# Turning more score blocks in place of computing them, with z, q and the output buffers rearranged (gated attention and hypermixer MLP, one core)

## The chip, the cores and the metric

The kernel runs on one core of one Trainium2 chip. The metric is the device time of one execution in microseconds (us). The kernel before was timed three times: 807.54, 807.89 and 812.27 us, with a median of 807.89 us.

A core has five engines that run their own instruction lists in order: PE (TensorE, the matmuls), DVE (VectorE), ACT (ScalarE), POOL (GpSimd) and SP (SyncE, which here only issues DMA transfers). They meet through semaphores. A DMA that SP issues is run by 16 DMA engines; SP itself takes some time to issue it, and cannot issue the next before.

## The reference

There are 8 batches of 3200 rows. The first part is an attention without a softmax, and the second mixes its result with two projections of itself:

```python
scores = (1.0 / S) * np.matmul(z, z.transpose(0, 2, 1))   # z: 8 x 3200 x 64
attn = np.maximum(scores, 0.0) ** 2                       # 8 x 3200 x 3200
x = u * np.matmul(attn, v)                                # u, v, x: 8 x 3200 x 256
wq = x @ w_q                                              # 8 x 3200 x 64
wk = x @ w_k
mixed = np.einsum('bst,btd->bsd', scale * np.einsum('bsd,btd->bst', wq, wk), x)
out = np.maximum(mixed, 0.0) @ w_out                      # 8 x 3200 x 256
```

The scores are symmetric, since both factors are z. What is computed for (row block i, column block j) is, transposed, the block (j, i).

## The kernel before

**Tiles and groups.** A batch has 25 row tiles of 128 (`NT`). The columns are cut into seven groups, six of 512 and a last one of 128 (`widths`, `LASTG`). A score tile is one row tile against one group: 128 x 512. Two tiles share a pair: `scores` (L210) computes both with two matmuls that use the two halves of the PE's rows, into one PSUM tile `sc`. `first_stage` (L229 on ACT, L233 on DVE) takes max(x, 0) and scales into the fp32 tile `g`; `second_stage` (L246 on ACT, L248 on POOL) squares `g` into the fp16 tile `at`.

**Turned blocks.** `is_turned(gi, gj)` says which blocks are computed only once: those of group gi against the rows of a later group gj, where gj is at most `FAR = 2` groups on, or is the last group. `second_stage` gives each such pair of tiles to SP, which issues a DMA transpose (L267) into a tile `tt1`, `tt2` or `ttl`. When group gj's turn comes, its missing rows are read from there (`weights`).

**Steps.** The main loop (`while groups`) runs in steps, counted by `k`. A step computes three pairs of score tiles (two where it also mixes), runs the first stage of these, the second stage of the pairs of the step before, and then a share of the second product (L288: attn times v, 25 row tiles x 4 column blocks for a group of 512) with tiles that are two steps old (`LAG = 2`). A batch takes 21 steps, 169 steps in all. When a group closes, `gate` (L314, DVE) multiplies by u into `x_sb`, and `turn_x` (L326) has SP transpose it into `xT`.

**Keys and queries.** Five or more steps later, in a step that neither mixes nor follows another such step too closely (`key_due`), `keys_and_heads` projects the group (L336), ACT casts it into `qk` (L347: rows 0 to 63 are q, 64 to 127 are k), and SP transposes it into `kx` (L352). At the next such step, here called a key step, `double_keys_queries` copies q into the other half of `qk` by a DMA of SP (L360) and k into the other half of `kx` by POOL (L361), and `heads` (L367, PE) needs that `kx`. So the key transpose has from one key step to the next to land. Once a whole batch has its heads, `mix` (L415), `mix_out` (L427, ACT), `proj` (L440) and `proj_out` (L464, and L465 for the store) run for one of its groups every third step, during the next batch.

**z of the next batch** (`group_begun`): `load_z` (L130) loads all of it with a cast to fp16 by a DMA of POOL's queue, 3 steps after the batch's first group begins; `double_z` (L133, DVE) doubles it 6 steps later, and `turn_z` (L137) has SP transpose all 25 tiles in one instruction one step after that. v comes in five pieces of POOL's queue (L126).

**Order on SP.** SP has a plain list, in the order in which the loop calls it: in each step first what is due (`at_phase`: u, z), then q copies, then the transposes of the second stage, stores and key transposes. An instruction of SP that waits holds all that are behind it.

**Buffers.** `pg` has 8 buffers of 4 KB a partition, which `g` shares with the output tiles `fo` and `fs`. The 14 buffers of `pat` hold `at`.

Of the kernel before, what the change touches and what calls it, by code (L numbers as in the profile page):

```python
# [9 lines left out]
FP16 = mybir.dt.float16  # L10
# [6 lines left out]
def kernel(  # L17
# [10 lines left out]
    nc = tc.nc  # L28
# [13 lines left out]
    LAG = 2  # L42
    FAR = 2

# [14 lines left out]
    pu = ctx.enter_context(tc.tile_pool(name="pu", bufs=2))  # L59
    pg = ctx.enter_context(tc.tile_pool(name="pg", bufs=8))  # L60
    pat = ctx.enter_context(tc.tile_pool(name="pat", bufs=NAT))
# [22 lines left out]
    ZCH = [(0, 4), (12, 6), (18, 7), (4, 8)]  # L84
    ident = consts.tile([P, P], FP16, tag="ident", name="ident")
    z32 = {}
    zd0 = pz.tile([P, NT, 2, dqk], FP16, tag="zd", name="zd")
    vs[0] = pv.tile([P, NT, D], FP16, tag="v_sb", name="v_sb")
# [10 lines left out]
    def cast_first(c):  # L99
        n0, nn = ZCH[c]  # L100
        casts = [
            (nc.vector.tensor_copy, nc.scalar.copy),
            (nc.scalar.copy, nc.gpsimd.tensor_copy),
            (nc.gpsimd.tensor_copy, nc.gpsimd.tensor_copy),
            (nc.gpsimd.tensor_copy, nc.gpsimd.tensor_copy),
        ][c]
        for half, cast in enumerate(casts):
            cast(out=zd0[:, n0 : n0 + nn, half, :], in_=z32[n0][:])

    def turn_first(c):  # L110
        n0, nn = ZCH[c]
        if c < 2:
            tp = acc_tile(c, "ztp", FP16)
        else:
            tp = pps.tile([P, 4 * W], FP16, tag="ps", name="ztp")
        for i in range(nn):
            nc.tensor.transpose(  # L117
                tp[:, ts(i, P)], zd0[:, n0 + i, :, :].rearrange("p a k -> p (a k)"), ident
            )
        copy = nc.scalar.copy if c == 1 else nc.vector.tensor_copy  # L120
        copy(out=zT[0][:, ds(n0 * P, nn * P)], in_=tp[:, 0 : nn * P])
# [5 lines left out]

    def load_z(b):
        zds[b] = pz.tile([P, NT, 2, dqk], FP16, tag="zd", name="zd")
        nc.gpsimd.dma_start(out=zds[b][:, :, 0, :], in_=rows(z, b))  # L130

    def double_z(b):
        nc.vector.tensor_copy(out=zds[b][:, :, 1, :], in_=zds[b][:, :, 0, :])  # L133

    def turn_z(b):
        zT[b] = pzt.tile([P, S], FP16, tag="zT2", name="zT2")
        nc.sync.dma_start_transpose(  # L137
            out=zT[b][:].rearrange("p (n s) -> p n s", s=P),
            in_=zds.pop(b)[:].rearrange("p n a k -> p (n a k)"),
        )  # L140
# [6 lines left out]

    wq32 = consts.tile([P, ND, dh], FP32, tag="wq32", name="wq32")
    wk32 = consts.tile([P, ND, dh], FP32, tag="wk32", name="wk32")
    wqk = consts.tile([P, ND, 2, dh], FP16, tag="wqk", name="wqk")  # L150
    wq2 = consts.tile([P, ND, 2, dh], FP16, tag="wq2", name="wq2")
    wk2 = consts.tile([P, ND, 2, dh], FP32, tag="wk2", name="wk2")
    wo = consts.tile([P, ND, D], FP16, tag="wo", name="wo")
    wo32 = {}

    def load_weights():
        wo32[0] = px.tile([P, ND, D], FP32, tag="x_sb", name="wo32")
        nc.sync.dma_start(out=wq32[:], in_=moe_w_q.rearrange("(c p) h -> p c h", p=P))
        nc.sync.dma_start(out=wk32[:], in_=moe_w_k.rearrange("(c p) h -> p c h", p=P))
        nc.sync.dma_start(out=wo32[0][:], in_=moe_w_out.rearrange("(c p) e -> p c e", p=P))  # L160

    def cast_weights():
        nc.gpsimd.tensor_copy(out=wqk[:, :, 0, :], in_=wq32[:])
        nc.gpsimd.tensor_copy(out=wqk[:, :, 1, :], in_=wk32[:])
        for half in range(2):
            nc.gpsimd.tensor_copy(out=wq2[:, :, half, :], in_=wq32[:])
            nc.gpsimd.tensor_copy(out=wk2[:, :, half, :], in_=wk32[:])
        nc.gpsimd.tensor_copy(out=wo[:], in_=wo32[0][:])

# [5 lines left out]

    def is_turned(gi, gj):
        return gi < gj and (gj <= gi + FAR or gj == LASTG)

# [7 lines left out]
    for b in range(B):  # L186
        for gi in range(NG):
            near = [t for t in range(NT) if is_turned(gi, group_of(t))]
            own = [
                t for t in range(NT) if t not in near and not is_turned(group_of(t), gi)  # L190
            ]
            if b == 0 and gi == 0:
                order = [t for n0, nn in ZCH for t in range(n0, n0 + nn)]
                assert sorted(order) == sorted(near + own)
            elif len(tiles) % 2:
                order = own[:1] + near + own[1:]
            else:
                order = near + own
            tiles += [(b, gi, t) for t in order]
            ends[b, gi] = len(tiles)  # L200
# [38 lines left out]
    def second_stage(p0, g, on_act):  # L239
# [11 lines left out]
        for tile_ in tiles[p0 : p0 + 2]:  # L251
            b, gi, ti = tile_
            made[tile_] = (at, at0)
            gj = group_of(ti)
            if is_turned(gi, gj):
                blocks.append((b, gi, gj, ti - starts[gj] // P, 1, at0, at0 + widths[gi]))
            at0 += widths[gi]
        if len(blocks) == 2 and blocks[0][:3] == blocks[1][:3] and blocks[1][3] == blocks[0][3] + 1:
            blocks = [blocks[0][:4] + (2, blocks[0][5], blocks[1][6])]
        for b, gi, gj, n0, nn, c0, c1 in blocks:  # L260
            if (b, gi, gj) not in turned:
                kind, nr, bufs = ("l", 1, 8) if gj == LASTG else (gj - gi, 4, gj - gi + 2)
                turned[b, gi, gj] = ptt.tile(
                    [P, nr, 4, P], FP16, tag=f"tt{kind}", name=f"tt{kind}", bufs=bufs
                )
            out = turned[b, gi, gj][:].rearrange("p n j t -> p (n j) t")
            nc.sync.dma_start_transpose(out=out[:, 4 * n0 : 4 * (n0 + nn), :], in_=at[:, c0:c1])  # L267
# [55 lines left out]
    def turn_x(b, gi):  # L323
        nn = widths[gi] // P
        xTs[b, gi] = pxt.tile([P, 4, ND, P], FP16, tag="xT_sb", name="xT_sb")
        nc.sync.dma_start_transpose(  # L326
            out=xTs[b, gi][:, 0:nn, :, :].rearrange("p n a s -> p (n a) s"),
            in_=xs[b, gi][:, 0:nn, :].rearrange("p n d -> p (n d)"),
        )
# [14 lines left out]
    def projections_out(b, gi, out):  # L344
        gw = widths[gi]
        qks[b, gi] = pq.tile([P, W], FP16, tag="qk", name="qk")
        nc.scalar.copy(out=qks[b, gi][:, 0:gw], in_=out)  # L347
# [8 lines left out]

    def double_keys_queries(b, gi):
        gw = widths[gi]
        nn = gw // P
        nc.sync.dma_start(out=qks[b, gi][dh:P, 0:gw], in_=qks[b, gi][0:dh, 0:gw])  # L360
        nc.gpsimd.tensor_copy(out=ks[b, gi][:, 0:nn, 0, :], in_=ks[b, gi][:, 0:nn, 1, :])  # L361
# [87 lines left out]
    def proj_out(b, gi, src, ways):  # L449

        n0 = starts[gi] // P
        fo = pg.tile([P, 2, W], FP32, tag="g", name="fo")
        flat_out = fo[:].rearrange("p a w -> p (a w)")
# [49 lines left out]
    def side_proj_out(b, ps):  # L503
        fo = pg.tile([P, 2, W], FP32, tag="g", name="fs")
        nc.scalar.mul(out=fo[:, 0, 0:D], in_=ps[:, 1, D : 2 * D], mul=FINAL_SCALE)
        nc.sync.dma_start(out=rows(out, b)[:, NT - 1, :], in_=fo[:, 0, 0:D])

# [3 lines left out]

    def due(k, fn):
        at_phase.setdefault(k, []).append(fn)

# [9 lines left out]
    def keys_and_heads(b, gis):  # L524
# [15 lines left out]
        if keyed:  # L540
            hb, hgis = keyed.pop(0)
            heads_out(hb, hgis, ps)
            if hgis[-1] == LASTG:
                todo_mix.extend((hb, i) for i in range(LASTG))
                side.append((side_mix, side_mix_out, hb))
        if aside:
            aside[1](aside[2], ps)
# [3 lines left out]
    def group_begun(k, b, gi):  # L551
# [4 lines left out]
        if gi == 0 and b + 1 < B:  # L556
            later = 4 if b == 0 else 0
            due(k + later + 3, lambda: load_z(b + 1))
            due(k + later + 9, lambda: double_z(b + 1))
            due(k + later + 10, lambda: turn_z(b + 1))  # L560
            for i in range(5):
                due(k + later + 5 + 3 * i, lambda i=i: load_v(b + 1, 5 * i, 5))

# [33 lines left out]
    while groups:  # L597
# [17 lines left out]
        if keying and keyed:  # L615
            for g_ in keyed[0][1]:
                double_keys_queries(keyed[0][0], g_)
        if mixing:
# [3 lines left out]
        for i, (p0, sc) in enumerate(fresh):  # L622
            on_act = i == act_pair and not mixing
            staged.append((p0, first_stage(p0, sc, on_act)))
        if k < 3:
            turn_first(k + 1)
# [86 lines left out]
    for g_ in hgis:  # L713
        double_keys_queries(hb, g_)
    psh = ps_tile("hd")
    heads(hb, hgis, psh, stop=False)
    last_gram(last, LASTG, psg)
    g32 = pg.tile([P, ND * D], FP32, tag="g", name="G")
# [4 lines left out]
    last_heads(last, g32, psh)  # L723
    heads_done(last, psh[:, 1, 0:D])
    for mb, mg in todo_mix[2:]:
        mix_out(mb, mg, mix(mb, mg))
# [53 lines left out]
```

## Time and profile before

| | |
|---|---|
| three runs, us | 807.54, 807.89, 812.27 |
| profiled execution, us | 811.74 |
| its span (first to last instruction), us | 810.0 |
| busy us: PE, DVE, ACT, POOL | 790.2, 492.0, 475.1, 485.5 |
| score matmuls (L210) | 920, busy 130.6 us |
| matmuls of the second product (L288), all three sources | 5000 |
| DMA transposes issued by SP: `tt`, `ttl`, `xT_sb`, `kx`, `zT` | 146, 48, 56, 54, 7 |
| granted TensorE clock | 1.00 throughout |

The profiled execution is 3.85 us longer than the median of the three runs, about as long as the slowest. Busy time of the PE is a sum over stretches in which at least one matmul was in flight. A row of the page's fifth part gives a group of instructions: line, engine, operation, output and inputs, count, then busy time and mean length of one, then the idle time of that engine just before and what ended it.

### The profile page before, as it was taken

How to read it: one execution, taken by the hardware profiler on the slowest of the kernel's cores; microseconds unless marked ns; L12 is line 12 of the kernel's file. 1: busy time of each engine (PE TensorE's matmuls, PEld its weight loads, DVE VectorE, ACT ScalarE, POOL GpSimd, SP SyncE). 2: the span in 40 equal slices, each digit the busy share in tenths (PEclk: the TensorE clock that was granted, in tenths of full speed). 3: DMA queues.
4: the chain of work that ended last, by engine and by line, in shares of the span. 5: the costliest groups of instructions: out<-in, count | busy, mean ns of one | idle time of the engine just before them, and what ended most of it. 6: DMA issues, size and time to landing. Idle time of an engine off the chain costs nothing.

```text
span 810.0 us, 16777 instructions
## 1 busy us (share of the span) xinstructions
PE 790.2 (98%) x6778; PEld 585.3 (72%) x6778; DVE 492.0 (61%) x514; ACT 475.1 (59%) x526; POOL 485.5 (60%) x352
## 2 busy tenths in 40 slices
PE   7999999999999999999999999999999989999996
PEld 4777777777777777777777777777777757767774
DVE  5766666656665556745666556755666646655525
ACT  6655555556665556555665556656665555565534
POOL 7966676564766457745666466764666555655410
PEclk9999999999999999999999999999999999999999
DMA  7999899997999969998999979999899996868536
GB/s 174 153 206 187 140 177 169 207 195 133 216 148 193 206 169 177 149 231 172 187 153 212 198 156 176 178 210 178 188 200 151 174 221 138 157 136 194 119 95 247
DMA packets 330877, 143.20 MB, mean 177 GB/s; under 512 B 307440, under 2 KB 313136, under 8 KB 330800
## 3 DMA queue, kind: packets, MB, share of 16 engines
q1 hardware_dynamic: 302528, 125.90, 76.5%
q0 software_dynamic: 28128, 15.98, 18.6%
q8 instruction: 53, 0.87, 0.5%
q14 instruction: 24, 0.20, 0.1%
q10 hardware_dynamic: 144, 0.26, 0.1%
HBM read 59.38 MB, written 26.21 MB: 106 GB/s over the span
## 4 chain that ended last, share of the span: by engine, by line
PE 91%; DMA 3%; DVE 2%; ACT 1%; issue 1%; SPq 1%; POOL 1%; DVEq 0%; POOLq 0%; ACTq 0%
PE acc L288 65%; PE sc L210 13%; PE fo L440 5%; PE qk L336 3%; PE qk L367 2%; DMA out_dram<-fo 2%; PE mx L415 2%; DVE g L233 1%; SPq L267 1%; POOL at L248 1%; ACT at L246 1%; PE ztp L117 0%; DMA xT_sb<-x_sb 0%; DVE x_sb L314 0%; DMA z<-in_z_dram 0%
## 5 line engine op out<-in xcount | busy, mean ns | idle before, releaser
L248 POOL TENSOR_TENSOR at<-g 128x1024 f16<-128x1024 f32 (+2 forms) x234 | 430.5, 1855 | 213.8 <-DVE g L233 124.5
L233 DVE TENSOR_SCALAR g<-sc 128x1024 f32<-128x1024 f32 (+1 forms) x340 | 388.1, 1184 | 193.9 <-PE sc L210 157.3
L288 PE MATMUL acc<-v_sb,at 128*128 128x256 f16 x3656 | 446.8, 273 | 0.4 <-DVE x_sb L314 0.4
L288 PEld LDWEIGHTS <-at 128*128 128x128 f16 x3656 | 344.7, 98 | 107.4 <-issue 66.6
L229 ACT ACTIVATE g<-sc 128x1024 f32<-128x1024 f32 x128 | 131.2, 1025 | 199.0 <-PE sc L210 186.7
L246 ACT ACTIVATE at<-g 128x1024 f16<-128x1024 f32 (+2 forms) x234 | 236.9, 1029 | 0.6 <-DVE g L233 0.6
L288 PE MATMUL acc<-v_sb,tt 128*128 128x256 f16 x1152 | 149.1, 273 | 0.0
L210 PE MATMUL sc<-zT 64*128 64x512 f16 x920 | 130.6, 382 | 4.6 <-DVE g L233 2.1
L288 PEld LDWEIGHTS <-tt 128*128 128x128 f16 x1152 | 112.5, 98 | 12.9
L314 DVE TENSOR_TENSOR x_sb<-acc,u_sb 128x512 f16<-128x512 f32 (+1 forms) x104 | 69.3, 668 | 66.9 <-PE acc L288 62.8
L427 ACT ACTIVATE rt<-mx 128x1024 f16<-128x1024 f32 (+1 forms) x49 | 49.1, 1012 | 56.8 <-PE mx L415 55.3
L210 PEld LDWEIGHTS <-zT 64*128 64x128 f16 x920 | 35.2, 95 | 53.4 <-issue 30.8
L361 POOL COPY kx<-kx 128x256 f16<-128x256 f16 (+1 forms) x54 | 20.1, 377 | 78.5 <-DMA kx<-qk 74.8
L464 ACT ACTIVATE fo<-fo 128x1024 f32<-128x1024 f32 (+1 forms) x40 | 40.6, 1014 | 27.2 <-PE fo L440 26.0
L440 PE MATMUL fo<-wo,rt 128*128 128x256 f16 x386 | 49.6, 273 | 1.9 <-ACT rt L427 1.0
L347 ACT CAST qk<-qk 128x512 f16<-128x512 f32 (+1 forms) x54 | 28.7, 545 | 28.5 <-PE qk L367 13.2
L440 PEld LDWEIGHTS <-rt 128*128 128x128 f16 x386 | 37.2, 98 | 7.8 <-ACT rt L427 2.2
L380 DVE TENSOR_TENSOR ha<-ha,qk 128x256 f32<-128x256 f32 x31 | 13.1, 421 | 30.1 <-ACT qk L347 30.1
L367 PE MATMUL qk<-x_sb,kx 128*128 128x256 f16 x191 | 28.4, 273 | 2.7 <-POOL kx L361 2.7
L336 PE MATMUL qk<-xT_sb,wqk 128*128 128x512 f16 (+1 forms) x108 | 29.9, 358 | 0.2
L367 PEld LDWEIGHTS <-kx 128*128 128x128 f16 x195 | 19.0, 98 | 15.0 <-POOL kx L361 3.2
L288 PE MATMUL acc<-v_sb,ttl 128*128 128x256 f16 x192 | 22.6, 273 | 0.0
(47 smaller groups left out, 149.4 us busy)
## 6 DMA issues: line engine op xcount, KB each, us to landing
u_sb<-in_u_dram SPq DMA_DIRECT2D x48, 512.0 KB, 4.8
out_dram<-fo SPq DMA_DIRECT2D x46, 512.0 KB, 4.3
v_sb<-in_v_dram POOLq DMA_DIRECT2D x35, 320.0 KB, 6.2
qk<-qk SPq DMA_DIRECT2D x47, 64.0 KB, 4.2
zd<-in_z_dram POOLq DMA_DIRECT2D x7, 400.0 KB, 8.0
tt<-at SPq DMA_TRANSPOSE x146, 4.5
u_sb<-in_u_dram SPq DMA_DIRECT2D x8, 128.0 KB, 3.1
xT_sb<-x_sb SPq DMA_TRANSPOSE x56, 3.9
```

Of the source, the lines that this page charges most:

```text
L210: nc.tensor.matmul(out=sc[:, h, 0:gw], lhsT=zT[b][half : half + dqk, ts(ti, P)], rhs=zT[b][half : half + dqk, ds(gs, gw)], start=True, sto ...
L229: nc.scalar.activation(out=g[:, hs, 0:w], in_=sc[:, hs, 0:w], func=RELU, scale=GSCALE)
L233: nc.vector.tensor_scalar(out=g[:, hs, 0:w], in0=sc[:, hs, 0:w], scalar1=0.0, scalar2=GSCALE, op0=AOP.max, op1=AOP.mult,)
L246: nc.scalar.square(out=out, in_=g[:, hs, 0:w])
L248: nc.gpsimd.tensor_mul(out=out, in0=g[:, hs, 0:w], in1=g[:, hs, 0:w])
L288: nc.tensor.matmul(out=accs[j // 2][:, ds((j % 2) * D, D)], lhsT=weights(b, gi, ti, j), rhs=vs[b][:, ti, :], start=(first and ti == rows_[ ...
L314: nc.vector.tensor_mul(out=xs[b, gi][:, 2 * half : 2 * half + n, :].rearrange("p n d -> p (n d)"), in0=accs[half][:, 0 : n * D], in1=us[b, ...
L336: nc.tensor.matmul(out=out, lhsT=w[:, ac, :, :].rearrange("p t h -> p (t h)"), rhs=xTs[b, gi][:, 0 : gw // P, ac, :], start=(start and ac ...
L367: nc.tensor.matmul(out=ps[:, 1, 0:D], lhsT=ks[b, gi][:, n, :, :].rearrange("p a h -> p (a h)"), rhs=xs[b, gi][:, n, :], start=((gi, n) == ...
L427: nc.scalar.activation(out=rts[b, gi][:, :, 0:gw], in_=ps[:, :, 0:gw], func=RELU)
L440: nc.tensor.matmul(out=banks[jf // 2][:, ds((j - jf) * D, D)], lhsT=rt[:, dc, ts(j, P)], rhs=wo[:, dc, :], start=(dc == 0 and j == jf), st ...
L464: nc.scalar.mul(out=flat_out[:, sl], in_=part, mul=FINAL_SCALE)
```

## The change

- `is_turned` takes the batch too: in all batches but the last a block three groups on is turned as well, which adds the blocks (0,3), (1,4) and (2,5) and a third kind of tile, `tt3`. The numbers of buffers are 3, 4 and 3.
- The order of the tiles within a group changes: the tiles of the next group come first, then the group's own, then the other turned ones; tile 24 is put first or last, so that pairs stay together.
- z of the next batch is loaded as fp32 by SP in four pieces (6, 6, 6 and 7 tiles), each cast twice by DVE two steps later, after the first stages of that step (`late`), and turned by SP one step after that.
- q is copied into its other half by DVE (`double_queries`), before the group is mixed, and not by SP.
- Outputs have buffers of their own (`pfo`); `g` has 7 buffers and shares them only after the main loop. `xT` and `qk` of the last group get small buffers of their own, and the weights are staged in `px`.

```diff
-    def is_turned(gi, gj):
-        return gi < gj and (gj <= gi + FAR or gj == LASTG)
+    def is_turned(b, gi, gj):
+        far = 3 if b + 1 < B else 2
+        return gi < gj and (gj <= gi + far or gj == LASTG)
...
-            elif len(tiles) % 2:
-                order = own[:1] + near + own[1:]
             else:
-                order = near + own
+                single = [NT - 1]
+                order = [t for t in near if group_of(t) == gi + 1 < LASTG]
+                order += [t for t in own + near if t not in order + single]
+                order = single + order if len(tiles) % 2 else order + single
...
-    def load_z(b):
-        zds[b] = pz.tile([P, NT, 2, dqk], FP16, tag="zd", name="zd")
-        nc.gpsimd.dma_start(out=zds[b][:, :, 0, :], in_=rows(z, b))
+    def load_z(b, i):
+        n0, nn = ZP[i]
+        z32[b] = pz.tile([P, 7, dqk], FP32, tag="z32", name="z32")
+        nc.sync.dma_start(out=z32[b][:, 0:nn, :], in_=rows(z, b)[:, n0 : n0 + nn, :])
...
+        for half in range(2):
+            nc.vector.tensor_copy(out=zds[b][:, 0:nn, half, :], in_=z32[b][:, 0:nn, :])
...
-        nc.sync.dma_start(out=qks[b, gi][dh:P, 0:gw], in_=qks[b, gi][0:dh, 0:gw])
+    def double_queries(b, gi):
+        gw = widths[gi]
+        nc.vector.tensor_copy(out=qks[b, gi][dh:P, 0:gw], in_=qks[b, gi][0:dh, 0:gw])
...
-        fo = pg.tile([P, 2, W], FP32, tag="g", name="fo")
+        if groups:
+            fo = pfo.tile([P, 2, W], FP32, tag="fo", name="fo")
+        else:
+            fo = pg.tile([P, 2, W], FP32, tag="g", name="fo")
...
-            due(k + later + 3, lambda: load_z(b + 1))
-            due(k + later + 9, lambda: double_z(b + 1))
-            due(k + later + 10, lambda: turn_z(b + 1))
+            for i in range(4):
+                due(k + later // 4 + 2 + 3 * i, lambda i=i: load_z(b + 1, i))
+                due(k + later // 4 + 4 + 3 * i, lambda i=i: double_z(b + 1, i), late)
+                due(k + later // 4 + 5 + 3 * i, lambda i=i: turn_z(b + 1, i))
             for i in range(5):
-                due(k + later + 5 + 3 * i, lambda i=i: load_v(b + 1, 5 * i, 5))
+                due(k + later + 3 + 3 * i, lambda i=i: load_v(b + 1, 5 * i, 5))
```

## The prediction

> **What bounds the kernel now.** I read the page's busy times first, then the groups of instructions, then the waits, then SP's own timeline.
>
> ```profile
> span 810.0 us, 16777 instructions
> PE 790.2 (98%) x6778; PEld 585.3 (72%) x6778; DVE 492.0 (61%) x514; ACT 475.1 (59%) x526; POOL 485.5 (60%) x352
> ...
> L210 PE MATMUL sc<-zT 64*128 64x512 f16 x920 | 130.6, 382 | 4.6 <-DVE g L233 2.1
> ...
> L361 POOL COPY kx<-kx 128x256 f16<-128x256 f16 (+1 forms) x54 | 20.1, 377 | 78.5 <-DMA kx<-qk 74.8
> ```
>
> The PE is busy 98% of the span, and none of the other three engines is near that. So what takes matmuls away shortens the kernel, as long as nothing else falls behind. The last row shows what is nearest to that: POOL stood 74.8 us for key transposes. The list of waits says how often, and who else waits:
>
> ```profile
> POOL kx L361 <- DMA kx<-qk: 74.8, 19, 9.4
> ...
> DVE g L233 <- DMA out_dram<-fo: 21.9, 7, 5.2
> ...
> PE qk L367 <- POOL kx L361: 2.7, 1, 2.7
> ...
> PE sc L210 <- DVE g L233: 2.1, 3, 0.8
> ```
>
> Each line gives the total in us, the number of times and the longest. Key transposes were late for POOL 19 times, and late for the PE once, by 2.7 us. So the slack is nearly spent. The reason is in SP's timeline of the third batch (start, time, instructions merged):
>
> ```profile
> 210.08 4.51 SPq L267 DMA_TRANSPOSE tt<-at  x2
> ...
> 224.52 10.71 SPq L267 DMA_TRANSPOSE tt<-at  x4
> ...
> 239.27 2.50 SPq L352 DMA_TRANSPOSE kx<-qk  x1
> ...
> 246.77 5.05 SPq L137 DMA_TRANSPOSE zT<-zd  x1
> ...
> 278.28 0.63 SPq L145 DMA_DIRECT2D u_sb<-in_u_dram  x1
> ```
>
> Between 210 and 279 us of that batch each instruction starts 0.1 us after the one before has ended: SP is never idle. It is the second bound of this kernel, for some 60 of a batch's 98 us. What it costs to issue is in the views of the tiles `tt` and `qk` (least, median and longest, ns):
>
> ```profile
> L267 SPq DMA_TRANSPOSE tt<-at x146: 1212/1290/6540, 20.5 to 750.5; - x146
> L352 SPq DMA_TRANSPOSE kx<-qk x54: 1108/1223/3109, 53.7 to 779.0; - x54
> L360 SPq DMA_DIRECT2D qk<-qk x54: 467/554/1582, 65.7 to 789.7; - x54
> ```
>
> A transpose takes SP 1.29 us, and longer where the DMA engines are full: the 146 sum to 250.4 us, a mean of 1.72. In the stretch above the mean is 1.84.
>
> **Part by part.**
>
> *Turned blocks.* Three block pairs of four tiles in seven batches are 84 score tiles less (920 to 836), and 169 steps become 155. L210 is busy 130.6 us for 920, or 0.142 us each with two in flight: 84 x 0.142 = **11.9 us less on the PE**. DVE, ACT and POOL lose 84/920 of their stages: about 35, 34 and 39 us, off the path and worth nothing by themselves.
>
> *Output buffers.* The 21.9 us that DVE stood for a store's landing end, since `g` no longer waits for stores. The PE's own row gives 2.1 us for waits on DVE before scores: **2.1 us less**.
>
> *q and z on DVE.* 54 copies and 56 casts are added; one doubling in seven batches (8.4 us) goes. Nearest rows: the doubling took 0.58 us alone and up to 2.19 us, and the first cast of 128x256 took 0.29 us. At some 0.38 us that is 42 us on DVE, against 35 + 8 us less: no change to its 61%. I take 0; hidden by DVE's 157 us of waits for scores. A cast that waits for late z would hold gates and first stages behind it. Its z is issued two steps earlier (8 to 11 us), SP is up to 12 us late, and the first loads of z landed in 2.1 to 5.4 us, so this can be late by about 5 us in the same stretch where SP is late anyway; I count it in the next part and let the upper end carry the rest.
>
> *SP's list.* I counted SP's instructions in the built program's order for groups 0 to 3 of the third batch (62.8 us before, 196.8 to 259.6), where the load is. Each price has 0.1 us added for the gap.
> - Transposes of `at`: 18 become 26. 8 x 1.82 = +14.6.
> - z transposes: one of 5.05 becomes three pieces (the fourth falls in group 4) of 6 tiles, nearest to the 8-block `tt` at its median: 3 x 1.39 - 5.15 = -1.0.
> - z loads: 4 x 0.52 = +2.1 (the first loads took 0.40 to 0.43). One more store: +0.5.
> - q copies: 5 less, mean 0.66 (31.2 us for 47): -3.8.
> - z by POOL's queue: its 128-byte packets ran from 209 to 214 us, and the two transposes beside and behind them took 3.18 and 2.19 us against 1.25: -2.8.
> Sum +9.6 us. The PE's time for these groups shrinks by 0.8 us (13 tiles for 17 in group 3), so SP has 10.4 us more to make up. From 196 to 210 us SP stood idle for 5.5 us in pieces; if it can use all of it, it ends about **5 us later** than before against the PE.
>
> What is late then is a key transpose. In batches three to six the one in group 2 was issued 10.4, 13.2, 10.1 and 10.9 us after the start of its key step, mean 11.2. That cost nothing, since the next key step came 25 us later. In the changed program key steps come every third step nearly throughout; here these have 6, 6 and 7 row tiles, and such steps took 4.3 (with keys), 4.1 (with a mix) and 3.9 us: 12.3 us. How late an issue may be: 13.7 us was just met with 15.3 us to the next key step, and at 640 us the same 13.7 with 14.5 made the PE wait 2.7. So about 1.5 us less than the distance: 10.8 here. With 5 us more, 16.2 - 10.8 = 5.4 us of waiting; as part of the 5 us is issued behind that transpose, I take 4 us a batch. The first batch has no stores or mixes yet, and the eighth turns no more than before: six batches, **24 us more**. Bounds: at the unloaded 1.39 in place of 1.82 the sum is 6.2 and the lag 1.5 us, a wait of about 1.7 us a batch, 10 us in all; at the saturated 1.94 and with nothing saved on z, some 10 us a batch, 60 us, though each wait gives SP time to catch up. And 0, if transposes of keys now stand earlier in the list than I count.
>
> **Sum.** 811.7 - 11.9 - 2.1 + 24 = 821.7 us for the profiled execution. That stands 3.85 us above the median of the three runs, so 818 us in their terms.
>
> **Rivals.**
>
> *The backlog is absorbed.* Turned tiles of the next group come first in a step's list now, one 5 us transpose and POOL's slow z are gone, and SP issues for only 623 of 810 us. Then only the gain stays: 807.9 - 14 = 794 to 799. Against it stands that groups 0 to 3 hold nearly all that is added, and that groups 4 to 6 get none of it. Point at which it decides: a key transpose issued under about 11 us after its step's start. Chance 0.25.
>
> *The new copies of DVE collide with POOL.* Three of the seven doublings took 0.58 us with POOL idle; the four that met a multiply of POOL's took 0.95 to 2.19, and two of those multiplies 2.20 in place of 1.88. A mean of 0.61 us more on 110 copies is 67 us on DVE, 492 to 559 us, and 7 us of POOL. If a tenth or so of it comes before a gate or a first stage that the PE needs, that is 7 to 10 us: 794 + 10 = 804, no measurable change. The Trainium skill, SBUF — State Buffer, Who interferes with whom, has this as a rule that speaks against the move: VectorE in its two-port modes (copies and casts among them) and GpSimd exclude each other, and the second to start waits for the whole instruction. The doublings agree with that, 2.19 us beside a multiply of 1.88; whether the new casts run in such a mode no run here shows yet. Chance 0.08.
>
> *SP and the DMA engines saturate.* The 84 tiles bring 43,008 packets of 256 bytes (302,528 on SP's queue before); in the table by windows the DMA share over groups 1 to 3 of the third batch is 0.85, 1.07 and 1.09 already (packets in flight overlap, so it can pass 1). If issue goes to 1.94 us throughout, half of the 60 us above arrives: 830 to 850. Chance 0.25.
>
> **Chances.** The forecast (811 to 828) has 0.42, of which 0.27 lies above 816 and 0.15 within 1% of 807.9. About 1% either way is what a measurement of this kernel can tell from no change, as the runs lie 4.4 us apart. Faster by over 1%: 0.25, from the first rival. Within 1%: 0.15 + 0.08 = 0.23. Slower: 0.27 + 0.25 = 0.52. The range runs from 795 to 842 us and leaves out the best of the first rival and the worst of the third. The signs are mixed; the forecast's own range is 811 to 828.
>
> **What would show it.** Right: L210 falls to 836 matmuls and about 119 us; the PE's waits for `kx` by POOL (L361) grow from 2.7 us to over 15; SP without idle time from group 0 to group 4; DVE's waits for stores gone. Wrong: PE waits for `kx` near zero and a span near 798 (absorbed), or waits of the PE on `g` and `x_sb` with copies of q and z of 1 us and more (the collision). A wait of DVE's casts for z would be a step that I counted in the wrong place.

## The result, and the profile after

The changed kernel takes 863.24 us (median of 6 runs, 857.52 to 870.62) against 807.71 us (median of 6, 806.06 to 812.27): 1.0656 times as long, with a 95% interval from 1.0626 to 1.0687. I had forecast 818 us and a range up to 842. The direction was right, the size was not: 55 us instead of 10. Times here and below are medians of all runs of a kernel, while ratios leave out a run that lies over 1.5% above the kernel's fastest (one each of after, `a_z_old`, `b_dummy8`, `a_24zact` and `a_ord2`), so that a difference of two times can be 2 us more than the ratios give: by the ratio, 53 us here.

The profiled execution after took 857.52 us, so it is the fastest of its six runs, 5.7 us under their median; what follows explains 46 of the 55 us. These lines of its page answer to those shown of before (busy time of each engine, then groups of instructions; a line number is now some 11 to 19 higher):

```profile
span 855.7 us, 16629 instructions
...
PE 796.6 (93%) x6694; PEld 590.0 (69%) x6694; DVE 533.3 (62%) x587; ACT 439.9 (51%) x495; POOL 437.8 (51%) x323
...
PEclk9999899999999899999999999999999999999999
...
L221 PE MATMUL sc<-zT 64*128 64x512 f16 (+1 forms) x836 | 120.4, 382 | 20.2 <-DMA zT<-zd 15.0
...
L380 POOL COPY kx<-kx 128x256 f16<-128x256 f16 (+1 forms) x54 | 21.0, 390 | 165.3 <-DMA kx<-qk 161.7
...
L376 DVE COPY qk<-qk 64x512 f16<-64x512 f16 x48 | 46.4, 972 | 1.2
...
L138 DVE CAST zd<-z 128x384 f16<-128x384 f32 (+1 forms) x56 | 31.6, 605 | 15.4 <-DMA z<-in_z_dram 15.3
```

The 84 score matmuls are gone (836), and the PE is still busy for 6 us more than before, in a span that is 46 us longer. POOL stands 161.7 us for key transposes, before 74.8. And two lines are new: VectorE's copies of q at 0.97 us each, and its casts of z, which themselves wait 15.3 us for z. The PE's own waits (total, times, longest) tell which of this reaches it:

```profile
PE sc L221 <- DMA zT<-zd: 15.0, 3, 6.6
PE qk L386 <- POOL kx L380: 13.9, 11, 2.9
PE acc L299 <- DVE x_sb L325: 8.5, 13, 2.7
PE mx L434 <- DVE qk L376: 3.9, 4, 1.8
PE sc L221 <- ACT rs L509: 3.8, 2, 3.3
```

Before, the largest but one of all such lines was the 2.7 us for `kx`. Now the PE waits 15.0 us for turned pieces of z, in three waits only; 13.9 us for doubled keys; and 8.5 us for gates, `x_sb`, which VectorE makes.

For the rest I took the start-to-start time of every pair of successive matmuls. Its median for the same two lines is the undisturbed pace; what a pair takes beyond it is a pause, or, where the trace's clock record reads 0.50, time lost to the clock. From the first matmul's start to the last's:

| us | before | after |
|---|---|---|
| undisturbed pace | 785.4 | 775.6 |
| pauses | 12.9 | 55.7 |
| lost at half clock | 0 | 14.2 |
| small differences | 2.4 | 0.9 |
| sum | 800.7 | 846.4 |

The removed matmuls are worth 9.8 us. Pauses cost 42.8 us more, nearly all in the five lines above, and the half clock 14.2 us that no line of waits shows. These are estimates: how the pairs are sorted moves pace and pauses by up to 7 us against each other, and the half clock by about 2.

### The profile page after: what moved, and what is told of

Read it like the earlier page. It is cut to its first block, busy times and chain, and to the rows that moved or that the text cites. A ratio compares the mean times of both kernels' runs of the same rounds, so it can differ in the third digit from the quotient of the medians.

```text
span 855.7 us, 16629 instructions
## 1 busy us (share of the span) xinstructions
PE 796.6 (93%) x6694; PEld 590.0 (69%) x6694; DVE 533.3 (62%) x587; ACT 439.9 (51%) x495; POOL 437.8 (51%) x323
## 4 chain that ended last, share of the span: by engine, by line
PE 72%; issue 8%; DMA 7%; DVE 5%; POOL 5%; SPq 1%; ACT 1%; DVEq 0%; POOLq 0%; ACTq 0%
PE acc L299 52%; PE sc L221 9%; PE fo L459 4%; POOL at L259 4%; PE qk L386 3%; DMA z<-in_z_dram 2%; DMA kx<-qk 2%; PE qk L350 2%; DVE g L244 2%; PE mx L434 1%; DMA zT<-zd 1%; DVE x_sb L325 1%; DVE qk L376 1%; DMA ttl<-at 1%; DVE zd L138 1%
## 5 line engine op out<-in xcount | busy, mean ns | idle before, releaser
L259 POOL TENSOR_TENSOR at<-g 128x1024 f16<-128x1024 f32 (+1 forms) x212 | 391.7, 1863 | 218.6 <-DVE g L244 111.3
L244 DVE TENSOR_SCALAR g<-sc 128x1024 f32<-128x1024 f32 (+2 forms) x309 | 356.3, 1194 | 167.6 <-PE sc L221 166.5
L299 PE MATMUL acc<-v_sb,at 128*128 128x256 f16 x3320 | 414.3, 276 | 8.8 <-DVE x_sb L325 8.5
L299 PEld LDWEIGHTS <-at 128*128 128x128 f16 x3320 | 316.3, 99 | 111.2 <-issue 71.0
L240 ACT ACTIVATE g<-sc 128x1024 f32<-128x1024 f32 (+2 forms) x117 | 116.0, 994 | 228.6 <-PE sc L221 219.5
L299 PE MATMUL acc<-v_sb,tt 128*128 128x256 f16 x1488 | 189.8, 276 | 0.0
L299 PEld LDWEIGHTS <-tt 128*128 128x128 f16 x1488 | 147.5, 99 | 18.9
L221 PE MATMUL sc<-zT 64*128 64x512 f16 (+1 forms) x836 | 120.4, 382 | 20.2 <-DMA zT<-zd 15.0
L380 POOL COPY kx<-kx 128x256 f16<-128x256 f16 (+1 forms) x54 | 21.0, 390 | 165.3 <-DMA kx<-qk 161.7
L221 PEld LDWEIGHTS <-zT 64*128 64x128 f16 x836 | 32.2, 95 | 69.2 <-issue 33.7
L376 DVE COPY qk<-qk 64x512 f16<-64x512 f16 x48 | 46.4, 972 | 1.2
L386 PE MATMUL qk<-x_sb,kx 128*128 128x256 f16 x191 | 29.6, 279 | 13.9 <-POOL kx L380 13.9
L138 DVE CAST zd<-z 128x384 f16<-128x384 f32 (+1 forms) x56 | 31.6, 605 | 15.4 <-DMA z<-in_z_dram 15.3
```

What stands on the lines that cost most here:

```text
L221: nc.tensor.matmul(out=sc[:, h, 0:gw], lhsT=zT[b][half : half + dqk, ts(ti, P)], rhs=zT[b][half : half + dqk, ds(gs, gw)], start=True, sto ...
L240: nc.scalar.activation(out=g[:, hs, 0:w], in_=sc[:, hs, 0:w], func=RELU, scale=GSCALE)
L244: nc.vector.tensor_scalar(out=g[:, hs, 0:w], in0=sc[:, hs, 0:w], scalar1=0.0, scalar2=GSCALE, op0=AOP.max, op1=AOP.mult,)
L259: nc.gpsimd.tensor_mul(out=out, in0=g[:, hs, 0:w], in1=g[:, hs, 0:w])
L299: nc.tensor.matmul(out=accs[j // 2][:, ds((j % 2) * D, D)], lhsT=weights(b, gi, ti, j), rhs=vs[b][:, ti, :], start=(first and ti == rows_[ ...
L376: nc.vector.tensor_copy(out=qks[b, gi][dh:P, 0:gw], in_=qks[b, gi][0:dh, 0:gw])
```

## Experiments

Each time below stands beside runs of the kernel before on the same chip (medians of 807.7 to 809.1 us); the ratio is to those. "Far" is how many groups ahead blocks are turned.

### Which part costs it: the third group, z, or q

Five kernels take the change apart. `a_far2` is after with

```
-        far = 3 if b + 1 < B else 2
+        far = 2
```

`a_z_old` is after with z by POOL's queue, one doubling and one transpose, as before. `a_far2_zold` has both. `a_q_sp` is after with q copied by a DMA of SP again (`nc.vector.tensor_copy` back to `nc.sync.dma_start`). `b_far3` goes from the other side, before with the third group and its buffers alone:

```
-        return gi < gj and (gj <= gi + FAR or gj == LASTG)
+        far = 3 if b + 1 < B else 2
+        return gi < gj and (gj <= gi + far or gj == LASTG)
...
-... (gj - gi, 4, gj - gi + 2)
+... (gj - gi, 4, [3, 4, 3][gj - gi - 1])
```

Expected:

> The changed kernel with blocks turned two groups on at most in every batch, as before; z, q, buffers and order stay changed. Backlog theory (84 tiles turned more put SP's list behind): SP has 42 transposes less, so the PE's waits for kx by GpSimd fall from 13.9 us to under 4 and the time to 800 to 812 us. Late-piece theory (the fourth z piece is turned too late for the first tiles of the next batch): PE waits for zT stay near 15 us and the time stays over 825. Collision theory (copies of q and casts of z on VectorE meet GpSimd's multiplies): those stay, time over 830.

> The kernel before with nothing changed but the blocks three groups on, turned in all batches but the last (and the buffers 3, 4, 3 for the turned tiles). Backlog theory: score matmuls fall to 836, but SP still copies q, POOL's queue still loads z and the 25-tile z transpose is still there, so SP is behind at least as much as in the changed kernel: 840 to 870 us, with PE waits for kx of 15 us or more. Late-piece and collision theories: neither cause is in it, so only the gain stays: 795 to 800 us.

> The changed kernel with z as before: one load with cast by POOL's queue three steps after the batch begins, one doubling by VectorE, one transpose of 25 tiles by SP ten steps after. Late-piece theory: the PE's 15 us of waits for zT go, with the slow clock that follows them about 22 us: 835 to 842 us. Backlog theory: SP's list gains little either way, so waits for kx stay at 10 to 25 us and the time at 840 to 865. Collision theory: 56 of 110 new VectorE copies go, a gain of 5 to 15 us.

> The changed kernel with q copied into its other half by SP as before, 54 transfers of 0.66 us, none by VectorE. Backlog theory: SP has 36 us more to issue, so waits for kx grow and the time rises to 865 to 890 us. Collision theory: VectorE loses 47 us of copies, waits for gates (x_sb, 8.5 us) fall by half or more and the time falls to 845 to 855.

> Leaves out of the change the third turned group (far 2 everywhere) and z's new path (z by POOL's queue whole, one doubling, one transpose); keeps q on VectorE, the outputs' own buffers and the new order of tiles. If the two parts are the whole loss and add up (-38.7 and -23 us, each measured singly): 801.5, between 798 and 806, so at or below the kernel before. If both singly removed the same lateness: 806 to 815, as the 13.9 us that the PE waits for x_sb in far 2 go and the rest is as before.

Measured:

| kernel | far | z | us | ratio, 95% interval |
|---|---|---|---|---|
| a_far2_zold | 2 | old | 811.6 | 1.0038 [1.0004, 1.0072] |
| a_far2 | 2 | new | 824.5 | 1.0204 [1.0176, 1.0233] |
| a_z_old | 3 | old | 840.2 | 1.0368 [1.0302, 1.0435] |
| after | 3 | new | 863.2 | 1.0656 [1.0626, 1.0687] |
| a_q_sp | 3 | new, q by SP | 872.5 | 1.0799 [1.0757, 1.0842] |
| b_far3 | 3 | old, all else as before | 831.3 | 1.0287 [1.0247, 1.0326] |

With the new order of tiles, which four of the five keep, the third group costs 28.6 us with z's old path and 38.7 with the new (27 and 37 by the ratios); z's new path costs 13.0 us at far 2 and 23.0 at far 3. q on VectorE, the outputs' buffers and the new order together cost at most 0.7% at far 2. And q on VectorE is not a loss in after but a gain of 9 us. The time of `a_far2_zold` was the rival's, not the sum: the two parts share 10 us. Two times lie outside all that was expected: `a_far2` between the ranges of the backlog and of the late pieces, and `b_far3` below the 840 of the backlog and far above the rival's 800. `a_z_old` lies in two of its ranges; its PE still waits 21.4 us for `kx`, and 5.0 for `zT`.

The PE's waits of `b_far3` say what the third group does by itself:

```profile
PE qk L368 <- POOL kx L362: 19.9, 9, 4.5
PE sc L211 <- DMA zT<-zd: 6.4, 1, 6.4
```

The first line is the mechanism that I had forecast, at 19.9 us instead of 24. But there is a late transpose of z with the old path too, 6.4 us in one wait, and 12.3 us at half clock, counted as above, at a pace of 774.2. So in time the third group alone costs 23.5 us net of some 11 us fewer matmuls, about 34 us where I had put 24.

### VectorE's casts and POOL's multiplies

In `a_far2` there is no wait for `kx` at all in the list; the PE waits for gates:

```profile
PE acc L299 <- DVE x_sb L325: 13.9, 19, 2.7
```

Why a gate is late is in the timelines of after (start, time, instructions merged), first VectorE's, then POOL's, then the PE's:

```profile
24.72 2.35 DVE L244 TENSOR_SCALAR g<-sc 128x1024 f32<-128x1024 f32 x2 [0.69 <-PE sc L221]
26.99 3.10 DVE L138 CAST zd<-z 128x384 f16<-128x384 f32 x2
30.02 1.28 DVE L325 TENSOR_TENSOR x_sb<-acc,u_sb 128x512 f16<-128x512 f32 x2
```

```profile
26.02 3.86 POOL L259 TENSOR_TENSOR at<-g 128x1024 f16<-128x1024 f32 x2 [0.51 <-DVE g L244]
```

```profile
30.75 0.38 PE L299 MATMUL acc<-v_sb,at 128*128 128x256 f16 x2 [2.67 <-DVE x_sb L325]
```

Two casts that take 0.35 us each at their quickest take 3.10 us here. POOL's two multiplies end at 29.88, the second cast at 30.09, the gate behind it runs, and the PE has stood for 2.67 us. The 48 copies of q in after show the same: the 10 that met no work of POOL's took 0.28 us on average, the 38 that met some 1.15 us, and 34 of those ended 0.14 to 0.15 us after an instruction of POOL's. Not every cast is held: those of six tiles (128x384) took 0.35 to 0.36 us where they met no work of POOL's and up to 2.05 beside it, but the 14 of the seven-tile piece (128x448) took 0.61 to 0.62 either way. To test it, `a_far2_zact` is `a_far2` with the casts on ScalarE:

```
-            nc.vector.tensor_copy(out=zds[b][:, 0:nn, half, :], in_=z32[b][:, 0:nn, :])
+            nc.scalar.copy(out=zds[b][:, 0:nn, half, :], in_=z32[b][:, 0:nn, :])
```

> After with far 2 everywhere (824.5 us) and the 56 casts of z by ScalarE in place of VectorE. In a_far2 the PE waited 13.9 us for x_sb, nearly each time behind a cast of z that took 1.1 to 2.0 us where it takes 0.35 alone and that ended 0.22 us after a multiply of POOL's. Theory 'VectorE's casts wait for POOL's multiplies, and the gates behind them are late': x_sb under 3 us, 809 to 814. Rival 'the pieces of z cost through SP's queue': stays at 820 to 826.

It takes 813.6 us, 1.0072 [1.0046, 1.0097], 10.9 us less than `a_far2`, and the wait is nearly gone:

```profile
PE acc L299 <- DVE x_sb L325: 1.7, 3, 1.3
```

So at far 2 casts on VectorE are nearly the whole price of z's new path. That it is POOL beside them, and not their place ahead of the gates alone, rests on the lengths above; no run takes POOL's work away from beside them. It is the rival that I had given 0.08. The Trainium skill, SBUF — State Buffer, Who interferes with whom, says that copies and casts that run in a two-port mode lock GpSimd out, or wait for it, for a whole instruction; 0.35 against up to 2.05 us for one cast agrees. The copies of q collide as much, but the PE waits for a copy of q only 3.9 us in all.

### Late pieces of z, and the order of tiles

The three waits for `zT` fall where the second, fourth and sixth batch begin. One of them, in the PE's timeline of after:

```profile
85.36 0.44 PE L221 MATMUL sc<-zT 64*128 64x512 f16 x3
91.69 1.03 PE L221 MATMUL sc<-zT 64*128 64x512 f16 x3 [5.88 <-DMA zT<-zd]
```

The new order puts tile 24 (`single`) first in group 0 of a batch that starts on an odd tile count. That tile lies in z's fourth piece, whose transpose is due only one or two steps earlier, when SP is behind with its list. With the old order, or at far 2, where a batch has two more steps, the piece has three or four steps in these batches. `a_24late` moves that tile alone:

```
-                order = single + order if len(tiles) % 2 else order + single
+                if gi == 0 and len(tiles) % 2:
+                    far_ = [t for t in near if group_of(t) not in (1, LASTG)]
+                    order = own[:1] + [t for t in order if t not in own[:1] + far_] + single + far_
+                else:
+                    order = single + order if len(tiles) % 2 else order + single
```

`a_ord` gives after the whole order of before (`own[:1] + near + own[1:]`, or `near + own`); `a_ord3` is that with z's old path, `a_ord2` that with far 2 as well, so the kernel before with q on VectorE, the outputs' buffers and the small moves alone (v's loads two steps earlier, small buffers for the last group, the weights' staging).

> Leaves nothing out; only the order of the score tiles differs from after: in group 0 of a batch that starts on an odd tile, tile 24 no longer comes first but behind the group's own and next-group tiles, so the fourth piece of z is needed one or two steps later. Theory 'the pieces of z come late' : the PE's 15.0 us of waits for zT (three times) go nearly to 0, and with them part of the 14 us at half clock that follow long waits: 840 to 850. Rival 'SP's list is late as a whole, and the PE would only wait at another place': waits for kx or x_sb grow by as much, within 5 us of 863.

> After (863.2 us) with the order of score tiles of the kernel before: near tiles first as they come, no tile 24 ahead of the others. If the new order is to blame for the three late pieces of z and for nothing else, as in a_24late: 843 to 852. If the new order also costs elsewhere (key transposes or turned tiles bunched): under 840. If it helps the turned tiles: over 855.

> Far 3 with z's old path, q on VectorE and the outputs' own buffers, but the order of tiles of the kernel before; so the third turned group alone (831.3 us) plus q and outputs, or a_z_old (840.2 us) less the new order. If q on VectorE takes 9 us off as it did in after, and the new order is what makes a_z_old slower than the third group alone: 820 to 828. If the order does nothing: 836 to 844.

> The kernel before with q on VectorE and the outputs' own buffers alone (far 2, z's old path, old order of tiles). If the new order costs something at far 2 as well, which hid a gain of q and outputs in a_far2_zold (811.6 us): 798 to 805, faster than both kernels. If q and outputs were simply covered before: 806 to 812.

| kernel | order | z | far | us | ratio, 95% interval |
|---|---|---|---|---|---|
| after | new | new | 3 | 863.2 | 1.0656 [1.0626, 1.0687] |
| a_24late | new, tile 24 later | new | 3 | 847.4 | 1.0480 [1.0433, 1.0527] |
| a_ord | old | new | 3 | 833.6 | 1.0301 [1.0283, 1.0318] |
| a_z_old | new | old | 3 | 840.2 | 1.0368 [1.0302, 1.0435] |
| a_ord3 | old | old | 3 | 838.0 | 1.0356 [1.0308, 1.0404] |
| a_ord2 | old | old | 2 | 814.6 | 1.0071 [1.0026, 1.0116] |

The order costs nothing that can be told with z's old path (840.2 and 838.0), and 30 us with its pieces. With the old order the pieces are no loss at all (833.6 against 838.0). So about half of the 55 us is neither the one nor the other but both. Of the 30 us, 16 go when tile 24 alone is moved (`a_24late`): there the order asked for the last piece first. The other 14 go only with the rest of the new order. The waits of `a_ord`, first two lines:

```profile
PE acc L296 <- DVE x_sb L322: 13.6, 18, 2.8
PE qk L383 <- POOL kx L377: 12.3, 11, 2.9
```

No `zT` any more, 4.3 us at half clock for 14.2, and pauses of 42.4 us for 55.7. In `a_24late` the line of `zT` is gone too, but `kx` grew:

```profile
PE qk L390 <- POOL kx L384: 23.0, 11, 5.9
PE acc L303 <- DVE x_sb L329: 8.1, 13, 2.7
```

I read this as the long waits for `zT` having given SP time to catch up; no run shows that apart. The other 14 us of the order's cost show in `kx` (23.0 to 12.3), but what in the order does it no run tells. My guess that q on VectorE would make `a_ord3` faster than the third group alone was a miss: 838.0 against 831.3. `a_ord2` was the other miss, a gain that isn't there.

### What is full: SP's list or the DMA engines

`b_dummy8` is the kernel before with 42 more transposes of 8 blocks, at the places at which after turns blocks three groups away, into a tile that nobody reads (a counter and a condition that always holds are left out here):

```
+        first_ = tiles[p0]
+        far_ = [t for t in tiles[p0 : p0 + 2] if group_of(t[2]) == t[1] + 3 < LASTG and t[0] + 1 < B]
+        if far_ and far_[0] == first_:
+            spare = ptt.tile([P, 8, P], FP16, tag="spare", name="spare", bufs=2)
+            nc.sync.dma_start_transpose(out=spare[:, 0 : NBLK, :], in_=at[:, 0 : NBLK * P])
```

`b_dummy1` sets `NBLK` to 1. `b_dummy_late` has the 42 of 8 blocks in groups 4 and 5, at every third pair of tiles. `a_actq` issues the loads of z and u and the stores by ScalarE's queue; its base is `a_24zact`, which is `a_24late` with z's casts on ScalarE.

> The kernel before with 42 more transposes of 8 blocks on SP's queue, at the places at which after turns the tiles of (gi, gi+3), into a tile that nobody reads; no score matmul is saved, no buffer of the others changes. Theory 'the SP backlog makes key transposes late': far 3 alone cost 23.5 us net of 11 us fewer matmuls, so 807.8 + 34: 835 to 850, with PE waits for kx of 15 to 25 us. Rival 'far 3 costs through its buffers or its order of tiles': within 5 us of 808.

> As b_dummy8, with 1 block in place of 8 in each added transpose: as many added instructions on SP, an eighth of the data. If SP's issue time is what counts (about 1.17 us for a small one against 1.29 to 1.8), most of b_dummy8's loss stays: 822 to 845. If the data on the DMA engines is what counts (transposes of all kinds stretched by each other), it falls away: 806 to 815.

> As b_dummy8 (before with 42 idle transposes of 8 blocks, +52 us), but with the same 42 spread over groups 4 and 5 of the first seven batches, every third pair of tiles, where the DMA engines and SP have room in the profile of before. Theory 'what counts is that groups 0 to 3 are full, not the sum over a batch': under 15 us of the 52 remain, 808 to 822. Rival 'the queue is short over the whole batch, wherever the work stands': over 30 us remain, 840 to 865.

> After (far 3) with tile 24 later, as in a_24late (847.4 us), and the casts of z by ScalarE. If the collision and late pieces are all that z's new path costs, it comes to the time with z's old path, 840 us: 835 to 843, with the wait for x_sb (8.1 us) nearly gone and kx still at about 20 us. If ScalarE, which now stands for late z in VectorE's place, holds its squares up: 846 to 856.

> As a_24zact, with the loads of z and u and the stores issued by ScalarE's queue in place of SP's: some 140 instructions of about 0.55 us leave SP's list, 75 us, about as much as the 42 added transposes brought (42 x 1.7 = 71). If SP's list is the bound that the third turned group runs into, its matmuls then pay: 800 to 815. If the data on the DMA engines is, little changes: 830 to 845. If issuing holds ScalarE up: over 845.

| kernel | us | ratio, 95% interval |
|---|---|---|
| b_dummy8 | 860.9 | 1.0638 [1.0604, 1.0672] |
| b_dummy1 | 830.7 | 1.0277 [1.0232, 1.0323] |
| b_dummy_late | 831.1 | 1.0286 [1.0269, 1.0303] |
| a_24zact | 848.0 | 1.0477 [1.0439, 1.0515] |
| a_actq | 870.0 | 1.0767 [1.0741, 1.0794] |

As many instructions with an eighth of the data cost 22 us, so the number of issues counts. The full data cost 30 us more. Whether that is the DMA engines or SP itself these two runs don't tell, since SP too takes longer: the 42 took 54.1 us to issue with one block and 72.5 with eight, and its instructions of all kinds sum to 661 and 696 us, before 623. In groups 4 and 5 the same transposes cost 23 us instead of 52: the first groups are the fuller ones, but there is little room anywhere. Two of these times were expected by neither theory: `b_dummy8` lies above the 835 to 850 of the backlog, and `b_dummy_late` between its two ranges. The idle transposes reach the PE by a second way beside `kx`. In the profile of `b_dummy8`, an execution of 878.5 us, the PE stood 15.0 us for `kx`, as the backlog had it, but 26.8 for `g`; in `b_dummy_late`, first the PE's two longest waits, then one of VectorE's:

```profile
PE sc L210 <- DVE g L233: 11.6, 6, 5.4
PE qk L380 <- POOL kx L374: 5.0, 2, 3.0
```

```profile
DVE g L233 <- DMA out_dram<-fo: 46.9, 13, 6.2
```

Stores land late (before, this line was 21.9 us), and in the kernel before `g` shares its buffers with them. That is what the outputs' own buffers spare the changed kernel, and where they would be worth something.

`a_actq` took 130 loads and stores, 78 us of issue, from SP. SP's transposes then grew from 580 to 636 us in sum (those of `at`, the last group's tiles included, from a mean of 1.60 to 1.78 us), so 55 of the 78 us were filled by longer transposes. And ScalarE was held up by issuing, the third case that I had named. Its list of waits has the first line below, and its timeline (an instruction that issues a DMA is marked ACTq) shows the longest of the seven:

```profile
ACT g L244 <- DMA tt<-at: 33.6, 7, 8.6
```

```profile
591.52 0.34 ACTq L152 DMA_DIRECT2D u_sb<-in_u_dram  x1
591.96 1.02 ACT L244 ACTIVATE g<-sc 128x1024 f32<-128x1024 f32 x1 [8.62 <-DMA tt<-at]
```

In all seven, a load or store that was moved to ScalarE stands right ahead of `g`, and it was this one that waited until a transpose of `at` had landed. So a shorter list of SP brought nothing here, but since ScalarE was held up as well, this run doesn't settle which of the two is full.

### Where the collision's time goes at far 3

`a_ord` still waits 13.6 us for gates. `a_ord_zact` and `a_ord_zpool` move its casts to ScalarE and to POOL.

> a_ord (after with the old order of tiles, 833.6 us) with the casts of z by ScalarE. There the PE waits 13.6 us for x_sb, 12.3 for kx and never for zT. If the collision of VectorE's casts with POOL is the next term, as at far 2 (-10.9 us): 819 to 826, so nearer to the kernel before but not at it, with kx at 10 to 20 us as what remains of the third turned group. If, as in a_24zact, ScalarE then stands for late z and passes the lateness on: 830 to 838.

> The same with the casts of z by POOL, whose own multiplies can't be beside them; the first casts by POOL took 0.50 to 0.62 us, so 56 of them are some 31 us for POOL, about as many as the 39 us of multiplies that the third turned group takes from it. If only the collision matters: 819 to 826. If POOL, which already stands 162 us for key transposes, is then late with its multiplies: 830 to 845.

They take 836.2 us, 1.0348 [1.0291, 1.0406], and 833.3 us, 1.0315 [1.0284, 1.0347]: no gain over the 833.6 of `a_ord`. The wait for gates falls to 1.7 and 1.6 us, and comes back as another, here of `a_ord_zpool`:

```profile
PE acc L296 <- POOL at L256: 15.0, 9, 7.1
PE qk L383 <- POOL kx L377: 13.0, 6, 3.8
```

```profile
POOL zd L138 <- DMA z<-in_z_dram: 158.1, 26, 10.6
```

With three groups turned z itself comes late, and whichever engine casts it stands for it and is late with its next work: POOL 158.1 us, ScalarE 41.5 us in `a_ord_zact`, VectorE 16.9 us in `a_ord`. These three are idle time of engines that are ahead of their work to a different degree, not three sizes of the lateness: POOL's stands for keys fell at the same time from 162.4 to 56.9 us. `a_24zact` had shown the same (848.0 against 847.4). At far 2 z is in time, and moving the casts pays.

No kernel of these is faster than the kernel before.

## Why the prediction was right or wrong

**Turned blocks: right.** L221 has 836 matmuls and 120.4 us, forecast about 119; the pace of all matmuls fell by 9.8 us, forecast 11.9.

**Output buffers: right in the trace, nothing in the time.** No line of VectorE waiting for stores is left. The 2.1 us that I subtracted can't be seen: `a_ord2` is not faster than before.

**SP's list: right in kind, and not the whole.** The PE's wait for `kx` grew from 2.7 to 13.9 us where I had put 24 us more and named 15 as the mark, so the sign just missed. But `b_far3`, which has this step alone, shows 19.9 us, and `a_24late` 23.0 without the waits for `zT`. So as a wait the term was about the right size for the third group; in after I take part of it to be covered by a worse wait. As a price in time it was too small: the third group alone lost about 34 us, since the half clock (12.3) and one late transpose of the whole z (6.4) come with it. SP is without idle time as forecast, and longer: in the third batch it issues for 92 to 96% of every 10 us from 220 to 290 us, groups 1 to 4; before, the stretch of 93% and more went from 210 to 270 us.

**"z transposes: … three pieces … -1.0" is the step that failed.** I priced the pieces by SP's time for them, and not by when each is needed. I had seen that z could come some 5 us late and said that SP's part counts it; the sum there has no such term. In after the fourth piece is turned one or two steps before tile 24 asks for it, and the PE stood 15.0 us in three waits, with the longest stretches of half clock behind two of them; with tile 24 later the waits are gone and the kernel takes 16 us less. That `single` stands ahead of the near tiles on odd starts is in the diff; I read it, and did not set it against the due steps of the pieces. What the order and the pieces cost together is 30 us by `a_ord`, more than the 11 to 20 that the late pieces alone were expected to give there; the cause of the 14 us beyond tile 24 stays open.

**"q and z on DVE … I take 0" failed too, for z.** The copies and casts took 0.97 and 0.61 us, not 0.38, since POOL's multiplies hold them up. I had this as a rival at 0.08, with 7 to 10 us; measured at far 2, it is 10.9 us; in after the wait for gates is 8.5 us, and with the third group moving the casts gained nothing. Its condition was right (a cast ahead of a gate that the PE needs), its chance was too low. The order of VectorE's instructions puts casts right ahead of gates: at far 2 the 42 six-tile casts took 49 us in sum, 34 more than at 0.35 each, and by the fall of the PE's wait for gates, from 13.9 to 1.7 us, some 12 of these reached the PE, not a tenth. For q the 0 was safe: on VectorE it saves 9 us of what the copies on SP cost in after. VectorE's wait for late z, 15.3 us, was named as the sign of a step counted in the wrong place; the sign came.

**Half clock: not in the sum at all.** I had put it at nothing without a reason; it is 14.2 us, a quarter of the loss.

**The rivals.** Absorbed (794 to 799): fell at once, since `kx` is late in all kernels with far 3. Saturation (830 to 850): nearest in time, and the dummies show that the queue has little room. But its mark, an issue time of 1.94 us with the gap of 0.1, so 1.84 without, didn't come: the mean for the transposes into `tt` is 1.70 us in after, 1.72 before. That the PE waits, so that fewer are issued in a given time, would explain it; no run shows it.

**The sum that the runs give:** before 808; the third group with q and outputs' buffers 838.0 (`a_ord3`); z in pieces 833.6 (`a_ord`); the new order but for tile 24 847.4 (`a_24late`); tile 24 first 863.2.

## What to carry to other kernels

When a transfer is split into pieces, write down for each piece the step at which it is issued and the step at which its first reader stands; the price of the pieces on the queue says nothing of the last one. Look at the order of readers in the same diff: two edits that are each harmless beside the third group cost 30 us together here. And a copy that is "free" on a half-idle VectorE is to be priced at the length of POOL's instruction beside it, as soon as anything urgent stands behind it.

## What the runs showed of the hardware

The PE's clock drops to half after short pauses. In the 16 of this study's 19 traces that have drops between the first and the last matmul, they start on a regular grid of 3.413 us, wherever the pauses lie, and each follows a stretch of the grid in which the PE was busy for under 48% of the time (0.479 was the highest). At full clock no stretch under 40% was without one; between 41 and 48% both occur. So some 1.8 us of pauses within one stretch can do it. In after, in the table by windows (PE busy and instructions, then those of PEld, DVE, ACT and POOL, then the granted clock, the DMA share and GB/s):

```profile
82.00:85.00 3.00, 3.00 (x30) 2.70 (x28) 1.87 (x2) 2.63 (x3) 0.00 (x0) 1.00 1.17 249
85.50:89.00 3.50, 0.31 (x3) 0.00 (x0) 1.23 (x1) 0.00 (x0) 0.00 (x0) 1.00 1.46 134
89.00:92.40 3.40, 0.71 (x3) 0.13 (x3) 0.00 (x0) 0.01 (x1) 2.27 (x3) 0.69 1.02 202
92.50:96.00 3.50, 3.50 (x15) 2.11 (x15) 1.22 (x1) 1.60 (x3) 3.50 (x2) 0.50 0.68 160
```

The wait for `zT` is in the second and third row, and the work behind it runs at 0.50: 15 matmuls in 3.5 us, where the first row has 30 in 3.0. A full stretch at half clock costs some 1.7 us more, and the PE counts as busy all the while, which is why its busy time grew. Eight such drops, two of them of two stretches, make the 14.2 us. The kernel before never falls under the mark within its body, `a_far2` once. The Trainium skill, TensorE: Matmul & The Clock Gate, Part 1: The HAM clock gate, has the free-running window of 3413 ns and the halved clock, which the traces agree with; its table lets the clock fall after an idle window, and here a window that was up to 48% busy was enough, so the measurement decides.
